# A fused attention and hard-swish kernel on one core: decay terms as columns, scores in halves, and another order of the second batch

## The chip, the core and the metric

The kernel runs on one core of a Trainium2 chip. The metric is the device time of one execution in microseconds (us). Before the change it is 375.04 us, the median of 3 runs (374.90 to 375.15). The profile shown below is of one execution, with a span of 374.1 us. TensorE (PE) multiplies matrices, PEld is its loading of the stationary operand, VectorE is DVE, ScalarE is ACT, GpSimd is POOL, and SP is the engine that issues most transfers.

## The reference, cut to what matters

Eight batches of eight heads each, 576 positions, 64 columns per head. A decay is added to the scores: the cumulative sum of max(s, 0) of the key minus that of the query. Then a causal softmax, and the product with v. The heads of a batch, side by side, are 576 rows of a 4608 x 512 matrix. It goes through two layers, 512 to 2048 and 2048 to 512, with a hard-swish between them.

```python
scores = (1 / np.sqrt(64)) * np.matmul(q, k.transpose(0, 1, 3, 2))
cum = np.cumsum(np.maximum(s, 0.0), axis=-1)
bias = -(cum[:, :, :, None] - cum[:, :, None, :])
scores = np.where(causal, -1e9, scores + np.minimum(bias, 0.0))
attn = softmax(scores)                                # rows sum to 1
x = np.matmul(attn, v).transpose(0, 2, 1, 3).reshape(4608, 512)
h = x @ w_in                                          # 512 x 2048
out = (h * np.clip(h + 3, 0, 6) / 6) @ w_out          # 2048 x 512
```

## The kernel before

Heads are handled in pairs: pair p has the heads 2p and 2p+1, and a batch is four pairs. For each pair q and k are loaded, cast to f16, transposed on TensorE and copied to `qkT`, 64 rows of data and 64 more rows. These extra rows carry the decay in three f16 parts, and rows of a table that keep masked blocks small. In the first pairs the decay rows come from a scan over all 64 heads:

```python
nc.sync.dma_start(out=s_sb, in_=s.rearrange("b h t -> (b h) t"))
nc.vector.tensor_scalar(out=s8, in0=s_sb, scalar1=0.0, scalar2=8.0, op0=ALU.max, op1=ALU.mult)
nc.vector.tensor_tensor_scan(out=c8, data0=s8, data1=s8, initial=0.0, op0=ALU.add, op1=ALU.max)
# ... [cut: c8 split into three f16 parts on DVE]
for hh in range(2):                                   # pair 0: row by row
    nc.sync.dma_start(out=kT[64:65, 0, c0:c1], in_=kaug[hh:hh + 1, 0, :])
    nc.scalar.dma_start(out=qT[67:68, 0, c0:c1], in_=qaug[hh:hh + 1, :])
    # ... [cut: two more parts]
# pairs 1 to 9: the rows go out to a scratch in DRAM and come back by load_aug(p)
```

Pairs 10 to 31 have the decay as columns beside q and k (`xb`, `decay_columns`), and a transpose by DMA. The scores of a head go through four PSUM banks, each with one exp on ACT and one mask on POOL. `attend` multiplies with v, in 15 matmuls of 65 columns. For an odd head it also divides by the row sums.

```python
def scores_bank(hd, bi):                              # four times per head
    S = psum.tile([128, 512], F32, tag="S", bufs=3)
    # ... [cut: one or two matmuls into S]
    nc.scalar.activation(out=P[:, p0:p0 + n], in_=S[:, 0:n], func=AF.Exp, scale=0.125, bias=0.0)
    mask(...)                                         # nc.gpsimd.affine_select on P

def attend(hd):
    # ... [cut: 15 matmuls of Pm with v_h into O]
    if hh == 1:
        nc.vector.reciprocal(out=r, in_=Ov[:, :, :, D:D + 1])
        nc.vector.tensor_tensor(out=xs..., in0=Ov[:, :, :, 0:D], in1=r..., op=ALU.mult)
```

A group of layer 1 (`m1(n, f)`) is four matmuls of 512 columns, a relu on ACT and one operation on DVE. A part of layer 2 (`m2(n, t4, part)`) is four such matmuls, and after the fourth part there is a copy and a store. A block n is 512 rows of the matrix, with 16 groups of layer 1 and 16 parts of layer 2.

```python
run(m1_0[:8])
weave(transposes(4) + pause + pause + block0_tasks(4), m1_0[8:14])
weave(block0_tasks(5), m1_0[14:] + m2_0[:4])
weave(block0_tasks(6) + [(decay_columns, 640), (copy_columns, 0)] + block0_tasks(7), m2_0[4:], 0.85)
weave(att_of[0], m1_tasks(1) + m2_of[1][:8])          # block 1; then one stage for each block
```

The first batch (pairs 0 to 3) runs ahead of `run(m1_0[:8])`. `block0_tasks(p)` is the attention of a pair p of the second batch: its eight score banks, the loads and casts for the pairs after it, both attends, the transposes of the next pair, and the transpose of its own result. `weave` spreads attention tasks between tasks of the layers. The layers' weights are loaded and cast by DMAs that POOL issues: w_in in two halves, within the first batch, and w_out in four pieces.

Of the kernel before, what the change touches and what calls it, by code (L numbers as in the profile page):

```python
# [16 lines left out]
def kernel(  # L17
# [33 lines left out]
    psum = ctx.enter_context(tc.tile_pool(name="psum", bufs=1, space=bass.MemoryType.PSUM))  # L51

    def bank():
        return psum.tile([128, 512], F32, tag="M", bufs=2, name="bank")

    ident_dram = nc.inline_tensor(np.eye(128, dtype=np.float16), name="ident_f16")
# [15 lines left out]
    NA = 8  # L72
    aug_drams = [
        nc.dram_tensor("aug_scratch0", (2, 4, NA * SEQ), F16, kind="Internal").ap(),
        nc.dram_tensor("aug_scratch1", (2, 4, (2 * PTD - NA) * SEQ), F16, kind="Internal").ap(),
    ]
# [3 lines left out]
    nc.scalar.preload_act_table_set("natural_log_exp_and_others")  # L80


    ident = cpool.tile([128, 128], F16, tag="c_id")
# [10 lines left out]
        cpool.tile([128, KC, 1024], F16, tag=f"c_win{h}", name=f"w_in{h}") for h in range(2)  # L94
    ]
    w_out_sb = cpool.tile([128, NF, DM], F16, tag="c_wout")


    amask = work.tile([128, 2, SEQ], F16, tag="amask", bufs=1)
    s_sb = work.tile([NH, SEQ], F32, tag="s0", bufs=1)  # L100
    nc.sync.dma_start(out=s_sb, in_=s.rearrange("b h t -> (b h) t"))
    nc.scalar.dma_start(out=amask[64:128], in_=amask_dram.ap().rearrange("i p t -> p i t"))
    nc.scalar.dma_start(out=ident, in_=ident_dram.ap())

    s8 = work.tile([NH, SEQ], F32, tag="s1", bufs=1)
    nc.vector.tensor_scalar(
        out=s8, in0=s_sb, scalar1=0.0, scalar2=8.0, op0=ALU.max, op1=ALU.mult
    )
    c8 = work.tile([NH, SEQ], F32, tag="s2", bufs=1)
    nc.vector.tensor_tensor_scan(  # L110
        out=c8, data0=s8, data1=s8, initial=0.0, op0=ALU.add, op1=ALU.max
    )

    aug = work.tile([NH, 2, 4, SEQ], F16, tag="s3", bufs=1)
    qaug, kaug = aug[:, 0, 3, :], aug[:, 1]
    nc.gpsimd.memset(warm, 0.0)
    nc.gpsimd.memset(aug[:, 0, 0:3, :], 1.0)
    nc.gpsimd.memset(aug[:, 1, 3, :], 1.0)
# [13 lines left out]
    def mask_rows(sl, copy):  # L132
        for i, dst in enumerate((kT, qT)):
            copy(
                out=dst[64:128, sl, 0:W2].rearrange("p (h t) -> p h t", h=2),
                in_=amask[64:128, i:i + 1, :].to_broadcast([64, 2, SEQ]),
            )


    qk_f = {}  # L140
    qk_h = {}
# [620 lines left out]
```

The softmax here doesn't subtract the row's maximum and nothing guards it: scores larger than these inputs give would overflow.

## Time and profile before

| engine | busy us | share of the span | instructions |
|---|---|---|---|
| PE | 354.2 | 95% | 2805 |
| PEld | 220.5 | 59% | 2805 |
| DVE | 190.4 | 51% | 331 |
| ACT | 209.8 | 56% | 405 |
| POOL | 149.1 | 40% | 378 |

| event | us from the start |
|---|---|
| first scores | 12.84 |
| last attend of the first batch begins | 33.21 |
| first group of layer 1 | 35.30 |
| transposes of pair 4 | 43.13 |
| first group of block 1 | 85.13 |

In the profile's lines a group of instructions is named by engine and line, then output <- inputs and the count. "bank L423" is layer 1, "po" or "bank L450" layer 2, "S L291" scores, "O L340" attend, "pT L247" transposes of q and k, "L378" transposes of the result, "pD L201" those of the decay, and "bank L490" matmuls with zeros that keep TensorE occupied. In the windows each row is a stretch of time, with each engine's busy time in it and, in brackets, the number of instructions; then the clock granted to TensorE, the share of time that the DMA engines were busy, and GB/s. In the waits, three numbers stand for the total in us, the count, and the longest. In the chain of work that ended last, a line is start, us, and what ran. A busy TensorE is not TensorE at its peak, since ends of matmuls are modelled and the matmuls overlap.

### The profile page before, as it was taken

The numbers are of one execution on the slowest core, as the hardware profiler recorded it, in microseconds if no ns is written. First come the engines' busy times: TensorE is split into PE (matmuls) and PEld (weight loads), VectorE is DVE, ScalarE is ACT, GpSimd is POOL, SyncE is SP. The second block draws the span as 40 slices with busy tenths as digits, with TensorE's granted clock in tenths as the row PEclk, the third lists the DMA queues.
The fourth block names the chain that finished last, engine by engine and source line by source line (L and its number), as shares of the span: only waits on it lengthen the run. The fifth ranks groups of instructions, "written<-read, shape, count | busy, mean of one in ns | idle before, by whom it ended". The sixth has DMA issues, their size and how long they took to land.

```text
span 374.1 us, 7656 instructions
## 1 busy us (share of the span) xinstructions
PE 354.2 (95%) x2805; PEld 220.5 (59%) x2805; DVE 190.4 (51%) x331; ACT 209.8 (56%) x405; POOL 149.1 (40%) x378
## 2 busy tenths in 40 slices
PE   6878879999999899999999999999999999999996
PEld 2455556556666566566656665666566655555544
DVE  5765856566642355345534553455345535554431
ACT  4464764336885677467746774677467714553310
POOL 5673344454666344444444444444444300000000
PEclk9999999999999999999999999999999999999999
DMA  9689999938899999899999989899995200011012
GB/s 162 137 155 210 205 218 204 237 108 180 157 190 197 231 172 235 188 232 198 198 208 222 206 177 234 194 196 180 213 194 112 56 31 28 28 39 46 28 58 84
DMA packets 184670, 59.36 MB, mean 159 GB/s; under 512 B 177856, under 2 KB 178336, under 8 KB 184632
## 3 DMA queue, kind: packets, MB, share of 16 engines
q1 hardware_dynamic: 182392, 54.28, 70.2%
q0 software_dynamic: 1680, 4.27, 6.4%
q8 instruction: 22, 0.36, 0.4%
q10 hardware_dynamic: 560, 0.32, 0.3%
q14 instruction: 16, 0.13, 0.1%
HBM read 37.49 MB, written 9.62 MB: 126 GB/s over the span
## 4 chain that ended last, share of the span: by engine, by line
PE 81%; DVE 5%; ACT 4%; DMA 4%; issue 2%; POOL 1%; SPq 1%; ACTq 0%; POOLq 0%
PE bank L423 26%; PE po L450 23%; PE S L291 10%; PE bank L450 7%; PE O L340 6%; PE bankS L423 4%; ACT Pm L299 3%; DMA qkT<-xb 2%; ACT trl L431 1%; DMA qkf<-in_k_dram 1%; DVE gT L432 1%; DVE qkT L262 1%; PE bank L490 1%; PE bankY L423 1%; DMA s_sb<-in_s_dram 1%
## 5 line engine op out<-in xcount | busy, mean ns | idle before, releaser
L299 ACT ACTIVATE Pm<-S 128x384 f16<-128x384 f32 (+2 forms) x256 | 115.5, 508 | 58.4 <-PE S L291 56.6
L432 DVE SCALAR_TENSOR_TENSOR gT<-trl,bank 128x512 f16<-128x512 f32 x123 | 84.5, 687 | 102.2 <-ACT trl L431 101.9
L304 POOL TENSOR_SCALAR_AFFINE_SELECT Pm<-Pm 128x128 f16<-128x128 f16 (+2 forms) x256 | 79.4, 312 | 132.7 <-ACT Pm L299 122.7
L431 ACT ACTIVATE trl<-bank,bias 128x512 f32<-128x512 f32 x123 | 85.2, 692 | 77.3 <-PE bank L423 75.5
L423 PE MATMUL bank<-xT,w_in 128*128 128x512 f16 x492 | 126.4, 382 | 0.7
L450 PE MATMUL po<-w_out_sb,gT 128*128 128x512 f16 x416 | 104.3, 379 | 0.0
L423 PEld LDWEIGHTS <-w_in 128*128 128x128 f16 x576 | 78.5, 146 | 33.3 <-issue 2.4
L450 PEld LDWEIGHTS <-gT 128*128 128x128 f16 x560 | 50.7, 98 | 46.8 <-issue 0.3
L291 PE MATMUL S<-qkT 128*128 128x320 f16 (+4 forms) x448 | 70.2, 261 | 6.8 <-ACT Pm L299 3.4
L291 PEld LDWEIGHTS <-qkT 128*128 128x128 f16 x448 | 41.0, 98 | 36.4 <-issue 3.6
L340 PEld LDWEIGHTS <-Pm 128*128 128x128 f16 x960 | 38.3, 97 | 13.4 <-POOL Pm L304 1.8
L340 PE MATMUL O<-v_h,Pm 128*128 128x65 f16 x960 | 40.8, 193 | 1.5 <-POOL Pm L304 1.3
L450 PE MATMUL bank<-w_out_sb,gT 128*128 128x512 f16 x144 | 35.8, 379 | 0.0
L352 DVE TENSOR_TENSOR xs<-O,r 128x640 f16<-128x640 f32 x32 | 26.4, 824 | 1.1
L459 DVE TENSOR_SCALAR osb<-po 128x512 f32<-128x512 f32 x26 | 17.9, 688 | 15.2 <-PE po L450 14.9
L222 POOL CAST xb<-qkf 128x1152 f16<-128x1152 f32 x22 | 25.3, 1150 | 0.0
L238 POOL CAST v_h<-v_f 128x640 f16<-128x640 f32 x28 | 20.2, 720 | 3.0 <-DMA v_f<-in_v_dram 3.0
L459 DVE TENSOR_SCALAR osb<-bank 128x512 f32<-128x512 f32 x9 | 6.2, 691 | 23.2 <-PE bank L450 23.2
L176 POOL CAST t<-qkf 128x1152 f16<-128x1152 f32 x10 | 11.5, 1154 | 13.7 <-DMA qkf<-in_k_dram 13.7
L423 PE MATMUL bankS<-xT,w_in 128*128 128x512 f16 x64 | 16.4, 379 | 0.0
L431 ACT ACTIVATE trl<-bankS,bias 128x512 f32<-128x512 f32 x16 | 11.0, 688 | 8.0 <-PE bankS L423 8.0
L432 DVE SCALAR_TENSOR_TENSOR gT<-trl,bankS 128x512 f16<-128x512 f32 x16 | 11.0, 688 | 6.8 <-ACT trl L431 6.8
(55 smaller groups left out, 130.8 us busy)
## 6 DMA issues: line engine op xcount, KB each, us to landing
qkf<-in_q_dram SPq DMA_DIRECT2D x32, 288.0 KB, 4.2
qkf<-in_k_dram SPq DMA_DIRECT2D x32, 288.0 KB, 4.3
out_dram<-osb SPq DMA_DIRECT2D x35, 256.0 KB, 2.4
v_f<-in_v_dram SPq DMA_DIRECT2D x64, 128.0 KB, 4.0
w_in<-in_moe_w_in_dram POOLq DMA_DIRECT2D x2, 1024.0 KB, 12.8
w_out_sb<-in_moe_w_out_dram POOLq DMA_DIRECT2D x4, 512.0 KB, 7.3
v_f<-in_v_dram SPq DMA_DIRECT2D x32, 32.0 KB, 2.7
qkT<-xb SPq DMA_TRANSPOSE x22, 4.9
```

What stands on the lines that cost most here:

```text
L222: nc.gpsimd.tensor_copy(out=x.rearrange("p (i t) c -> p t i c", i=2)[:, :, :, 0:D], in_=qk_f.pop(p))
L238: copy(out=v_h[:, sl, :, :, 0:D], in_=v_f[:, sl])
L291: nc.tensor.matmul(out=S[:, c:c + hi - lo], lhsT=kT[:, sl, off + 128 * kt:off + 128 * (kt + 1)], rhs=qT[:, sl, off + lo:off + hi], start=( ...
L299: nc.scalar.activation(out=P[:, p0:p0 + n], in_=S[:, 0:n], func=AF.Exp, scale=0.125, bias=0.0)
L304: nc.gpsimd.affine_select(out=view, in_=view, pattern=pattern, compare_op=ALU.is_ge, fill=0.0, base=0, channel_multiplier=-1,)
L340: nc.tensor.matmul(out=O[:, hh, qt * VW:qt * VW + D + 1], lhsT=P[:, c:c + 128], rhs=v_h[:, sl, hh, kt, 0:D + 1], start=(qt == 0), stop=(qt ...
L352: nc.vector.tensor_tensor(out=xs.rearrange("p t h d -> p h t d"), in0=Ov[:, :, :, 0:D], in1=r.to_broadcast([128, 2, 5, D]), op=ALU.mult,)
L423: nc.tensor.matmul(out=ph, lhsT=w_in_t[f // 8][:, kc, f % 8, :], rhs=xT[:, kc, n * 512:(n + 1) * 512], start=(kc == 0), stop=(kc == KC - 1),)
L431: nc.scalar.activation(out=trl, in_=ph, func=AF.Relu, bias=bias3[:, 0:1], scale=1.0)
L432: nc.vector.scalar_tensor_tensor(out=gT[n][:, f, :], in0=trl, scalar=6.0, in1=ph, op0=ALU.min, op1=ALU.mult)
L450: nc.tensor.matmul(out=po, lhsT=gT[n][:, f, t4 * 128:(t4 + 1) * 128], rhs=w_out_sb[:, f, :], start=(f == 0), stop=(f == NF - 1),)
L459: nc.vector.tensor_scalar_mul(out=osb, in0=po, scalar1=1.0 / 6.0)
```

## The change

The aim is to start the first batch sooner, to take masks and small transfers out of it, and to have layers 1 and 2 of block 0 in another place. The parts:

- **Decay of the first batch as columns.** Only s of batch 0 is loaded at first, as 72 rows of 64. One short scan and four small matmuls with 0/1 tables give the cumulative sums, already transposed. They are written as columns beside q and k in a tile `x0`, and come out of the transposes as rows 64 to 67. The scan over all heads comes later, on POOL and DVE, for pairs 4 to 9 and the columns of the later pairs.
- **Scores in halves.** A head of the first batch has two halves of 896 and 704 columns, each over two PSUM banks with one exp. The causal mask is one more matmul for each diagonal block, of the identity with a triangle of -65504.
- **Weights in quarters.** w_in comes as four DMAs of 512 columns, and all eight weight DMAs are issued while head 5 is worked on. The columns of one stationary operand of w_in are now 4 elements apart, not 8.
- **Second batch beside layer 2.** All of layer 1 and the first half of layer 2 of block 0 run ahead of the second batch, without attention beside them. The second batch has the other 8 parts of layer 2.
- **PSUM by hand.** One tile of eight banks, with rings of bank numbers, in place of tagged tiles. Layer 1 of block 0 has a ring of six.

```diff
+    XW = 68
+    x0 = gT2[:, 1]...                       # [cut] pair, tile, q or k, 68 columns
+    def first_columns():
+        nc.vector.tensor_scalar(out=s_first, in0=s_first, ...)
+        nc.vector.tensor_tensor_scan(out=scan, data0=s_first, data1=s_first, ...)
+        # [cut] four matmuls with `sums` into cT
+        nc.vector.tensor_copy(out=hi, in_=c3)
+        nc.vector.tensor_tensor(out=r3, in0=c3, in1=hi, op=ALU.subtract)
+        # [cut] mid, lo and the negative of hi in the same way
+    def scores_half(hd, half):
+        # [cut] three matmuls of k and q, two or three of ident and tri
+        nc.scalar.activation(
+            out=Pm[:, hd % NS, p0:p0 + n], in_=S[:, 0:n], func=AF.Exp, scale=0.125, bias=0.0
+        )
-    w_in_t = [w.rearrange("p k (m f) -> p k f m", f=8) for w in w_in_sb]
+    w_in_t = [w.rearrange("p k (m f) -> p k f m", f=4) for w in w_in_sb]
-        copy = nc.vector.tensor_copy if p < 4 else nc.gpsimd.tensor_copy
-        copy(out=v_h[:, sl, :, :, 0:D], in_=v_f[:, sl])
+        nc.gpsimd.tensor_copy(out=v_h[:, sl, :, :, 0:D], in_=v_f[:, sl])
+    keep_warm(6)
+    first_columns()
+    mask_rows(0, 1, A.copy)
+    mask_rows(0, 0, G.tensor_copy)
+    # [cut] casts and turns of pair 0 in two pieces, on A, G and V
+    for hd in range(2 * FIRST):
+        scores_half(hd, 0)
+        # [cut] turn_first of q or k of the next pair, cast of the pair after it, loads
+        scores_half(hd, 1)
+        if hd > 0:
+            attend(hd - 1)
+        if odd and p > 0:
+            x_transpose(p - 1)
+        if hd == 5:
+            for c in range(4):
+                load_w_in(c)
+            for c in range(4):
+                load_w_out(c)
+    rows = decay_rows()
+    rows[0]()                                # POOL: memsets, product
+    attend(2 * FIRST - 1)
+    opened = [bank("A") for _ in range(4)]
+    # [cut] groups 0 to 3 of layer 1: kc 0 to 2 around x_transpose(3), then kc 3 and m1_act
+    rows[1]()                                # DVE: scan over all heads
+    rows[2]()                                # POOL: three f16 parts
+    store_aug(nc.sync)
+    for sl in (1, 2, 0):
+        for i in range(2):
+            mask_rows(sl, i, G.tensor_copy)
+    for p in range(FIRST, FIRST + 3):
+        load_pair(p)
-    run(m1_0[:8])
-    weave(transposes(4) + pause + pause + block0_tasks(4), m1_0[8:14])
-    weave(block0_tasks(5), m1_0[14:] + m2_0[:4])
+    run(m1_0[4:])
+    run(m2_0[:8])
+    cast_qk(FIRST)
+    cast_v(FIRST)
+    weave(transposes(4) + block0_tasks(4), m2_0[8:10])
+    weave(block0_tasks(5), m2_0[10:13])
     weave(
         block0_tasks(6) + [(decay_columns, 640), (copy_columns, 0)] + block0_tasks(7),
-        m2_0[4:],
+        m2_0[13:],
         0.85,
     )
```

## The prediction

> **What bounds the kernel now.** I read the windows first, cut at the borders of the stages, because the 95% of TensorE over the span hides where its idle time lies.
>
> ```profile
> core 0: us, PE busy (x) PEld busy (x) DVE busy (x) ACT busy (x) POOL busy (x), PEclk, DMA share, GB/s
> 0.00:12.80 12.80, 8.81 (x38) 3.72 (x39) 8.46 (x14) 4.17 (x4) 6.82 (x14) 1.00 0.78 133
> 12.80:35.30 22.50, 17.43 (x234) 12.37 (x233) 14.34 (x30) 13.32 (x32) 13.86 (x36) 1.00 0.92 181
> 35.30:43.10 7.80, 7.80 (x39) 5.08 (x37) 5.28 (x8) 5.44 (x8) 1.23 (x2) 1.00 0.93 188
> 43.10:85.10 42.00, 36.88 (x364) 23.38 (x364) 26.39 (x62) 19.08 (x41) 20.86 (x46) 1.00 0.94 197
> 85.10:122.40 37.30, 36.66 (x340) 24.43 (x339) 18.90 (x32) 27.15 (x57) 22.21 (x58) 1.00 0.96 175
> ...
> 160.10:197.90 37.80, 37.66 (x311) 23.84 (x310) 17.77 (x29) 24.49 (x48) 18.35 (x49) 1.00 1.12 212
> ```
>
> From 85.1 us on TensorE is full (37.66 of 37.80 us), and the change leaves that code alone but for the weights' layout. So the question is only when block 1 of layer 1 starts. Before that there are 12.8 us without scores, 22.5 us of the first batch, and 42 us of the second batch woven with layers 1 and 2 of block 0, where 5.1 us are idle. The waits of TensorE up to 36 us, and the longest early pieces of the chain, come second:
>
> ```profile
> PE pTm L247 <- POOL t L176: 2.7, 2, 1.7
> PE S L291 <- ACT Pm L299: 1.4, 6, 0.3
> ```
>
> ```profile
> 17.01 1.16 POOL t L176
> 18.27 5.15 DMA qkf<-in_k_dram
> 23.54 1.15 POOL t L176
> 32.51 0.86 PE bank L490 x4
> 35.47 1.79 PE bank L423 x8
> ```
>
> The first batch is held by GpSimd's cast of a pair, and that by a q/k load (5.15 us of the chain), while each head has four exps and four masks in sequence. Third, the timeline of TensorE from the attends of pair 6 to block 1, because it shows what a pair costs when little is woven in:
>
> ```profile
> 69.12 0.83 PE L340 MATMUL O<-v_h,Pm 128*128 128x65 f16 x15
> 69.80 1.02 PE L450 MATMUL bank<-w_out_sb,gT 128*128 128x512 f16 x4
> 70.66 0.67 PE L247 MATMUL pT<-ident,t 128*128 128x128 f16 x9
> 71.16 0.44 PE L378 MATMUL pT<-ident,xs 128*128 128x128 f16 x5
> 71.44 1.03 PE L450 MATMUL po<-w_out_sb,gT 128*128 128x512 f16 x4
> 72.63 0.65 PE L201 MATMUL pD<-ident,aug 64*128 64x64 f16 x10 [0.16 <-DVE qkT L262]
> 73.51 1.14 PE L201 MATMUL pD<-ident,aug 64*128 64x64 f16 x20 [0.23 <-DVE qkT L262]
> 74.58 1.04 PE L450 MATMUL po<-w_out_sb,gT 128*128 128x512 f16 x4
> 75.49 0.33 PE L291 MATMUL S<-qkT 128*128 128x256 f16 x2
> ...
> 85.13 1.03 PE L423 MATMUL bank<-xT,w_in 128*128 128x512 f16 x4
> ```
>
> [...] the 384-wide exp takes 494 ns, the 512-wide 598 ns, and four in a row (1600 columns) end 1.69 us after the first begins. [...] a group of four stands in the chain with 0.86 us. [...] Here 98 ns hold for gT, qkT and Pm, but 146 ns for w_in, whose columns lie 8 elements apart[...]. [...]
>
> **The change, part by part.**
>
> Start. The decay terms of pair 0 no longer go through row DMAs (the eight small ones are issued at 6.7 to 10.6 us) but come from one scan and four small matmuls into columns of x0. Only 18 KB of s are loaded for it, so I put those columns at about 5.6 us. The mask load is now third on its queue: I put it at 5.3 us (it ended the wait of ACT's mask copy at 4.66). Then on ACT a mask copy (1.15), a cast of about 0.45, five transposes and a copy of about 0.5 us on VectorE; ACT's k copy is about 0.7 us, later by a little. First scores at 8.4 instead of 12.84 us.
>
> First batch. Per head two exps of 896 and 704 columns[...]. The 1.5 us of masks on GpSimd go. TensorE gains two or three small matmuls per half for masks: scores take 0.48 + 0.43 us plus some gaps, about 1.0; attend 0.47 (15 in the chain); nine transposes for q or k 0.5; x_transpose 0.28. That is 2.0 us for an even head, 2.3 for an odd one, with turns; 1.5 and 1.7 in the last pair, whose successor is turned later. The sum without waits is some 16 us. The loads decide the middle: 4 pairs of 885 KB plus about 0.4 MB at the 205 GB/s that busy stretches show land pair 2's q and k at 13.5 us, pair 3's at 17.8, the last v at about 21. With a 1.15 us cast pair 3 is turned at 19; three and a half heads follow, so 26. GpSimd issues eight weight DMAs from about 20 (0.55 to 0.77 us each, 5 us) before it casts the v of pair 3, done at 25.7, when attend of head 6 wants it: up to 0.8 us. So layer 1 starts at 27 instead of 35.3, and the bubble after the last attend (1.17 us on xs) is filled by the four opened sums. Gain here: 8.3 us.
>
> Layer 1 of block 0 with half of layer 2, alone: 24 groups of 0.864 us, 20.7, so 48. Weights: the two halves landed 10.6 and 15.0 us after issue; a quarter at a time at that pace comes every 3 to 4 us from 23.5, and w_out is in by about 45. Both ACT and VectorE need 0.69 us per group, under 0.864, and six banks give slack for the scan (1.35) inserted on VectorE. GpSimd meanwhile: aug memsets and product 2.8, wait for the scan until about 35[...], six mask copies of 1.15 = 7, then casts 1.15 + 0.72: 48.4. This only just meets TensorE at 48.
>
> Second batch. It now has 8 groups of layer 2 beside it (6.9 us) instead of 23 (19.9). A pair has attention of about 3.7 us on TensorE, but its own chain is longer: first score to last attend 5.2 us (64.79 to 69.96, with one group inside), then reciprocal, xs and the first two copies of q and k on VectorE, 2.6 us (70.00 to 72.6), and the next scores. That is 7.8 us a pair where the woven groups fall into holes. Now it takes 9.7. Pair 4 also pays transposes and copies at its head, 2.4 us, so scores at 50.4. Pairs 5 and 6 begin at 58.3 and 66.7 (one group lies on the path in each). The decay columns lengthen pair 6 to pair 7: 5.5 us lie between 69.96 and 75.49, so pair 7 begins at 77.3. It needs 5.0 to its last attend, then a group, transposes and x_transpose, 2.0. Block 1 begins at 84.3 instead of 85.1. Idle TensorE in this stage: 36.3 us less 6.9, four times 3.7 and 1.5 of decay transposes, so 13 us, against 5.1 in the old stage.
>
> Sum. Of 8.3 us gained, some 7.5 are given back, because 15 groups have been moved out of the holes of the second batch. The weights' columns lie 4 elements apart instead of 8. Where a layer-1 group follows scores or attends it takes 0.90 us in the chain instead of 0.86; about half of the woven groups do. If the load gets shorter, up to 0.04 x some 70 = 2.8 us come over the rest of the kernel; I take half, 1.4, plus the 0.8: 2.2 to 3. Predicted: 372.0 us.
>
> **The rivals.** First: the early start survives. If woven groups, shorter waits of the pairs, or an x_transpose off the path hold the second batch to 31 us, block 1 starts at 79 to 80 and the time is near 368; a stride-free weight load takes it to 366.5. For it speaks that the S banks and ACT have no relu beside them now; against it that pair 6 of before already ran with few groups and still needed 5.2 + 2.6 us. Second: GpSimd becomes the bound. It carries casts of v that VectorE did, row operations, six mask copies and eight DMA issues; the 1.58 us of one VectorE subtraction that took 0.75 alone shows that they can disturb each other. If its chain ends at 52 instead of 48.4, all that follows moves: 375 to 376. Third: the transfers. DMA stands at 0.92 to 0.94 busy up to 85 us, so nothing done earlier helps if bytes arrive no sooner. But pairs 4 to 6 are asked for at about 40 us with the queue free, and pair 7 some 15 us later. Weights late by 5 us would give 377.
>
> **Range and chances.** The start of layer 1 I trust to 1.5 us, the second batch to 3, the weight load to 1.4; together about 3.6, leaning to the fast side. Range 366.5 to 377.5. Faster by over 2% means under 367.5, which needs nearly the whole early gain: 0.15. Slower by over 2% means over 382.5, two of the rivals against me: 0.05. Within: 0.80.
>
> **What the profile will show.** Right: first scores at 8 to 9 us, no affine select in the first batch, layer 1 from 26 to 28 us, then 20 us of full TensorE, then about 36 us at some 65% busy, block 1 at 83 to 86, and stages of 37.7 us or a little less after it, with weight loads of w_in under 146 ns. Wrong: block 1 near 80, TensorE waiting for the weights' DMA or for a GpSimd cast near 48, or waits in the later stages.

## The result, and the profile after

The changed kernel takes 376.79 us (median of 4 runs, 376.26 to 377.87) against 375.0 for the kernel before (4 runs, 374.9 to 375.15): ratio 1.0047, 95% interval 1.0029 to 1.0064. It is slower by half a per cent, where 0.8% faster had been predicted.

In what follows "block 1" as a moment is the start of the first group of layer 1 of block 1, and so on for the other blocks. A "hole" is a stretch in which TensorE waits for the chain of one pair, and in which a woven group can run. In the new kernel's lines L488 is layer 1, L527 layer 2, L330 scores of the second batch and later, L396 scores of the first batch, L418 attend, L286 transposes of q and k, L456 those of the result, L247 those of the decay, L567 zero matmuls. First the windows of the changed kernel, cut at its own borders (first scores, layer 1, block 1, block 2, block 3), columns as before:

```profile
core 0: us, PE busy (x) PEld busy (x) DVE busy (x) ACT busy (x) POOL busy (x), PEclk, DMA share, GB/s
0.00:10.22 10.22, 6.50 (x28) 2.76 (x28) 4.71 (x13) 3.58 (x4) 4.75 (x15) 1.00 0.93 183
10.22:28.75 18.53, 18.00 (x286) 15.10 (x287) 10.08 (x18) 12.96 (x16) 14.73 (x19) 1.00 1.00 188
28.75:84.68 55.93, 48.37 (x409) 28.11 (x406) 31.59 (x69) 23.77 (x48) 32.23 (x55) 0.97 0.89 186
84.68:123.29 38.61, 35.25 (x323) 21.50 (x321) 20.61 (x37) 26.98 (x56) 21.54 (x58) 1.00 0.83 164
123.29:160.88 37.59, 37.42 (x316) 21.91 (x312) 17.76 (x29) 24.48 (x48) 18.50 (x49) 1.00 1.17 217
```

The first batch starts 2.6 us sooner and TensorE is full in it (18.00 of 18.53 us): layer 1 starts 6.5 us sooner. From there to block 1 it takes 55.93 us instead of 49.83, with 7.6 us of idle TensorE instead of 5.1. The next row has 3.4 us of idle TensorE (35.25 of 38.61 us busy), in a stage that the prediction took to be full. The timeline of TensorE in the changed kernel shows where:

```profile
30.37 12.68 PE L488 MATMUL PS<-xT,w_in 128*128 128x512 f16 x58
43.68 7.93 PE L527 MATMUL PS<-w_out_sb,gT 128*128 128x512 f16 x36 [0.63 <-DVE gT L499]
51.45 0.67 PE L286 MATMUL PS<-idtri,t 128*128 128x128 f16 x9
52.98 0.56 PE L330 MATMUL PS<-qkT 128*128 128x256 f16 x4 [0.86 <-DVE qkT L301]
...
77.59 0.33 PE L330 MATMUL PS<-qkT 128*128 128x256 f16 x2 [0.76 <-DVE dec L262]
78.40 0.59 PE L330 MATMUL PS<-qkT 128*128 128x192 f16 x2 [0.48 <-DVE dec L260]
...
84.68 0.81 PE L488 MATMUL PS<-xT,w_in 128*128 128x512 f16 x3
87.24 0.38 PE L488 MATMUL PS<-xT,w_in 128*128 128x512 f16 x1 [1.75 <-DVE xT L464]
```

Four things stand in it. Layer 1 and half of layer 2 run without attention beside them from 28.75 to 51.45, with one gap between the layers. The two scores of 192 columns, 0.38 us elsewhere (at 90.66), take 0.59 at 78.40, where the granted clock is one half (0.50 in the windows, from 78.3 to 81.7). Block 1 begins at 84.68, but its fourth matmul comes at 87.24: it reads the transposed result of pair 7, whose copy stands on VectorE behind the four copies of pair 8. So block 1 really begins some 1.75 us later than its first line says. The borders of the traces, in us, beside those of two kernels from the experiments below:

| kernel | layer 1 | block 1 | block 2 | block 3 | span |
|---|---|---|---|---|---|
| before | 35.30 | 85.13 | 121.00 | 159.96 | 374.1 |
| after | 28.75 | 84.68 | 123.29 | 160.88 | 374.3 |
| e16_win | 30.27 | 84.44 | 121.28 | 158.87 | 372.0 |
| e18_ahead | 29.20 | 81.56 | 120.07 | 157.66 | 370.8 |

From block 3 on nothing differs but the weights' layout. (Before it, each kernel has waits of its own: before stands for 1.03 us at 125.3 for a transfer of `xb`, so block 3 is the border to compare.) The changed kernel is 0.92 us behind there and regains 0.75 by the end. (The profiled execution of before is a long one: a median of 375.0 less the 1.7 us that time and span differ by is 373.3.)

### The profile page after: what moved, and what is told of

Read it like the earlier page. It is cut to its first block, busy times and chain, and to the rows that moved or that the text cites. A ratio compares the mean times of both kernels' runs of the same rounds, so it can differ in the third digit from the quotient of the medians.

```text
span 374.3 us, 7691 instructions
## 1 busy us (share of the span) xinstructions
PE 355.0 (95%) x2852; PEld 206.8 (55%) x2852; DVE 184.0 (49%) x322; ACT 207.8 (56%) x389; POOL 158.3 (42%) x368
## 4 chain that ended last, share of the span: by engine, by line
PE 83%; ACT 5%; DVE 5%; issue 3%; DMA 2%; POOL 1%; POOLq 0%; ACTq 0%; DVEq 0%
PE PS L527 31%; PE PS L488 30%; PE PS L330 9%; PE PS L418 6%; ACT Pm L338 3%; DVE qkT L301 2%; PE PS L396 2%; DMA qkf<-in_q_dram 2%; ACT trl L498 2%; PE PS L732 2%; DVE gT L499 1%; PE PS L456 1%; PE PS L547 1%; POOL Pm L343 1%; PE PS L286 1%
## 5 line engine op out<-in xcount | busy, mean ns | idle before, releaser
L499 DVE SCALAR_TENSOR_TENSOR gT<-trl,PS 128x512 f16<-128x512 f32 x144 | 97.8, 685 | 105.7 <-ACT trl L498 105.6
L488 PE MATMUL PS<-xT,w_in 128*128 128x512 f16 x576 | 143.0, 379 | 2.6 <-DVE xT L464 1.7
L498 ACT ACTIVATE trl<-PS,bias 128x512 f32<-128x512 f32 x144 | 98.4, 691 | 81.7 <-PE PS L488 79.0
L527 PE MATMUL PS<-w_out_sb,gT 128*128 128x512 f16 x560 | 138.2, 379 | 0.6 <-DVE gT L499 0.6
L338 ACT ACTIVATE Pm<-PS 128x384 f16<-128x384 f32 x224 | 102.1, 507 | 57.0 <-PE PS L330 55.4
L343 POOL TENSOR_SCALAR_AFFINE_SELECT Pm<-Pm 128x256 f16<-128x256 f16 x224 | 68.8, 307 | 126.2 <-ACT Pm L338 117.5
L488 PEld LDWEIGHTS <-w_in 128*128 128x128 f16 x576 | 61.5, 114 | 46.3 <-issue 2.4
L527 PEld LDWEIGHTS <-gT 128*128 128x128 f16 x560 | 51.0, 98 | 49.3 <-issue 0.9
L330 PE MATMUL PS<-qkT 128*128 128x256 f16 x392 | 63.4, 265 | 5.2 <-DVE qkT L301 2.9
L330 PEld LDWEIGHTS <-qkT 128*128 128x128 f16 x392 | 36.9, 99 | 39.0 <-issue 9.3
L418 PEld LDWEIGHTS <-Pm 128*128 128x128 f16 x960 | 38.4, 98 | 13.6 <-POOL Pm L343 2.8
L536 DVE TENSOR_SCALAR osb<-PS 128x512 f32<-128x512 f32 x35 | 24.1, 688 | 43.3 <-PE PS L527 43.0
L418 PE MATMUL PS<-v_h,Pm 128*128 128x65 f16 x960 | 41.3, 193 | 2.2 <-POOL Pm L343 1.9
L430 DVE TENSOR_TENSOR xs<-PS,r 128x640 f16<-128x640 f32 x32 | 26.4, 824 | 1.1
L396 PE MATMUL PS<-qkT 128*128 128x64 f16 (+4 forms) x48 | 9.6, 292 | 1.0 <-ACT qkT L738 0.8
## 6 DMA issues: line engine op xcount, KB each, us to landing
w_out_sb<-in_moe_w_out_dram POOLq DMA_DIRECT2D x4, 512.0 KB, 16.5
```

The costliest lines, as they stand in the source:

```text
L330: nc.tensor.matmul(out=S[:, c:c + hi - lo], lhsT=kT[:, sl, off + 128 * kt:off + 128 * (kt + 1)], rhs=qT[:, sl, off + lo:off + hi], start=( ...
L343: nc.gpsimd.affine_select(out=view, in_=view, pattern=pattern, compare_op=ALU.is_ge, fill=0.0, base=0, channel_multiplier=-1,)
L418: nc.tensor.matmul(out=O[:, hh, qt * VW:qt * VW + D + 1], lhsT=P[:, c:c + 128], rhs=v_h[:, sl, hh, kt, 0:D + 1], start=(qt == 0), stop=(qt ...
L430: nc.vector.tensor_tensor(out=xs.rearrange("p t h d -> p h t d"), in0=Ov[:, :, :, 0:D], in1=r.to_broadcast([128, 2, 5, D]), op=ALU.mult,)
L488: nc.tensor.matmul(out=ph, lhsT=w_in_t[f // 4][:, kc, f % 4, :], rhs=xT[:, kc, n * 512:(n + 1) * 512], start=(kc == 0), stop=(kc == KC - 1),)
L498: nc.scalar.activation(out=trl, in_=ph, func=AF.Relu, bias=bias3[:, 0:1], scale=1.0)
```

## The experiments

Ratios are against the kernel before, run beside it on the same chip. The medians of the kernel before lie between 374.9 and 376.7 us from one experiment to another, and single runs spread over several us, so small effects are read from the borders in the traces. The trace of e10_half is of an execution that took 382.26 us, the longest of 14, so its borders are not compared.

**The start: is it TensorE's slow pace?** e1_warm doubles the zero matmuls that keep TensorE occupied.

```diff
-    keep_warm(6)
+    keep_warm(12)
-    keep_warm(4)
+    keep_warm(8)
```

> The changed kernel with 12 and 8 matmuls on zeros at the start instead of 6 and 4. Theory A (TensorE ran its first work at half clock: its 512-wide matmuls are 0.43 us apart up to 13.6 us and 0.22 after it): the first scores begin near 9.5 instead of 10.2 us, the 17 transposes after them take about 1.0 instead of 1.8 us, layer 1 begins 1.5 to 2.2 us sooner, at about 27, and the time falls to 374.6 to 375.3. Rival (the start waits for q, casts and loads whatever the clock is): layer 1 begins within 0.4 us of 28.9 and the time stays at 376.4 to 377.

Measured: ratio 1.008 [1.0051, 1.0109], first scores at 10.80, layer 1 at 29.06. The timeline of e1_warm:

```profile
6.63 0.45 PE L709 MATMUL PS<-sums,scan 72*64 72x36 f32 x4
...
9.22 0.75 PE L732 MATMUL PS<-idtri,gT 128*68 128x128 f16 x10
10.80 0.39 PE L396 MATMUL PS<-qkT 128*128 128x512 f16 x1 [0.83 <-ACT qkT L738]
```

The ten transposes take 0.75 us instead of 1.28. (In after a zero matmul of 512 columns takes 634 ns, one of layer 1 379; from the first scores at 10.22 to the next matmul it is 0.40 us, from those at 13.63 it is 0.22. The windows give a granted clock of 1.00 for this stretch too, so a half clock at the start is read from these times alone.) But all of them now stand behind zeros: the matmuls of the decay columns at 6.63 instead of 4.47, the transposes at 9.22 instead of 8.11. A pace that is bought in this way does not bring layer 1 forward; with it, layer 1 comes 18.26 us after the first scores instead of 18.53.

**The border between the layers.** The first part of layer 2 took a bank that a group of layer 1 still held (1.45 us between the last layer-1 and the first layer-2 matmul). e2_ring turns the ring of banks so that it is free.

```diff
-    "A": (3, 4, 5, 0, 1, 2)
+    "A": (5, 3, 4, 0, 1, 2)
```

> The changed kernel with the ring of layer 1 of block 0 turned by one place, so that the first sum of layer 2 gets a bank whose group was finished three groups earlier. Theory B (the 1.45 us between the last matmul of layer 1 at 42.2 us and the first of layer 2 at 43.68 is the wait for a PSUM bank that the last but one group holds): TensorE goes on without a gap, pair 4's transposes come 1.2 to 1.4 us sooner, unless GpSimd's cast (ends at 50.2 us) holds them, and the time falls by 1.0 to 1.4 us to about 375.5. Rival (layer 2 waits for the last gT itself): no change of the gap, 376.4 to 377.

Measured: ratio 1.0003 [0.9977, 1.0029]. Layer 2 follows without a gap at 43.20, and the transposes of pair 4 come 21.9 us after layer 1's start (50.97 less 29.05) instead of 22.7. It gives back 0.8 us.

**The copy ahead of block 1.** e3_xt puts the transposes of pair 7's result ahead of those of pair 8.

```diff
-            + transposes(p + 1)
-            + [(lambda: x_transpose(p), 640)]
+            + ([(lambda: x_transpose(p), 640)] + transposes(p + 1) if p == 7
+               else transposes(p + 1) + [(lambda: x_transpose(p), 640)])
```

> The changed kernel with the transposed result of pair 7 ahead of the transposes of pair 8. Theory C (the first group of block 1 stands 1.75 us because its last input is copied by VectorE behind four copies for pair 8): that wait goes, block 1 runs 1.0 to 1.8 us sooner, time 375.0 to 375.8. Rival (pair 8's scores then wait for the copies that have moved back, so nothing is gained): 376.3 to 377.

Measured: ratio 1.0035 [1.0008, 1.0063]. The wait of 1.75 is gone and the stage from block 1 to block 2 takes 37.10 instead of 38.61, but block 1 itself starts 0.5 later after layer 1 (56.4 against 55.9), since it now waits on the result itself. Net 1.0 in the trace; too little to show in the times.

**The weights' layout alone.** e4_quarters is the kernel before with w_in in four tiles, so that a matmul's columns lie 4 elements apart instead of 8.

> The kernel before with w_in in quarters, columns of a stationary operand 4 elements apart, and nothing else of the change. Theory D (the weight loads of w_in, 146 ns before and 114 ns after, are exposed where a group follows scores or attends): 1.0 to 2.0 us faster than before, 373.0 to 374.0, with stages of about 37.5 instead of 37.75 us. Rival (the loads lie under matmuls anyway, and what the changed kernel has gained behind block 1 has another source): 374.8 to 375.2.

Measured: ratio 0.9986 [0.9962, 1.0009]; stages of 37.59 instead of 37.75, span 373.31 instead of 374.10. The group of weight loads in before, then in e4_quarters (busy, then ns of one, then idle time):

```profile
L423 PEld LDWEIGHTS <-w_in 128*128 128x128 f16 x576 | 78.5, 146 | 33.3 <-issue 2.4
```

```profile
L420 PEld LDWEIGHTS <-w_in 128*128 128x128 f16 x576 | 61.3, 114 | 45.9 <-issue 2.9
```

The loads are busy for 17.2 us less in all, and the span is 0.8 shorter: nearly all of it lay beside matmuls. The interval of the ratio includes 1; what speaks for the 0.8 is that each stage is shorter by the same 0.16.

**The half clock.** e6_fill puts zero matmuls where TensorE is thin: seven and seven at the start, four after the decay columns, two and two about an attend of pair 6. e8_after is the changed kernel once more, beside it.

> The changed kernel with matmuls on zeros where TensorE idles: 7 and 7 instead of 6 and 4 at the start, and two each around the second attend of pair 6 and four after the decay transposes. Theory F (the halved clock costs time: it was granted at half up to 13.4 us and from 78.3 to 81.7): the clock is full from about 8 us on with no half stretch before the end, the transposes of pair 1 take about half as long, pair 7 from first score to last attend takes 4.7 instead of 5.45 us, and block 1 starts 1 to 2 us sooner. Rival (those stretches wait for loads, casts, exps and copies, and the clock does not matter there): block 1 starts within 0.5 us of 84.7 counted from the same start of layer 1, or later by what the zeros add.

> The changed kernel once more, unchanged, beside the three others and the kernel before: 0.3 to 0.7% above the kernel before, layer 1 from 28.8, block 1 from 84.7 us. It shows how far its stage borders and clock repeat.

Measured: e6_fill 1.0051 [1.0007, 1.0096], e8_after 1.006 [1.0019, 1.01]. In the traced run of e6_fill the granted clock from layer 1 to block 1 is 0.97, as in after, and block 1 comes 57.1 us after layer 1 instead of 56.0. Four other runs of e6_fill show a full clock (1.00) and took 376.13 to 377.16 us, where five runs of e8_after at 0.995 took 376.24 to 379.32, four of them 376.43 or less. So a full clock with zeros shows no gain; what the half clock costs by itself is not shown. The repeated kernel has a granted clock of 0.995 over its traced run, as after has. It also has a wait that the first trace of the same kernel lacks, near the end of block 1:

```profile
120.76 0.56 PE L330 MATMUL PS<-qkT 128*128 128x256 f16 x4 [1.48 <-DMA qkT<-xb]
```

It is for the transposed columns of a later pair, and the stage from block 1 to block 2 is 40.25 us long, against 38.61. The traces of e1_warm (1.6 us) and e18_ahead (1.5 us) have such a wait too.

**The order of the layers alone.** e7_order is the kernel before with the change's order: all of layer 1, eight parts of layer 2, then the second batch with the other eight. First batch and rows stay as they were; the four loads of the weights of layer 2 are asked for ahead of the casts of pair 4.

```diff
-    run(m1_0[:8])
-    weave(transposes(4) + pause + pause + block0_tasks(4), m1_0[8:14])
-    weave(block0_tasks(5), m1_0[14:] + m2_0[:4])
+    run(m1_0)
+    run(m2_0[:8])
+    weave(transposes(4) + block0_tasks(4), m2_0[8:10])
+    weave(block0_tasks(5), m2_0[10:13])
     # [cut] the last weave takes m2_0[13:] instead of m2_0[4:]; order of the w_out loads
```

> The kernel before with one part of the change alone: all of layer 1 and half of layer 2 of block 0 run ahead of the second batch, 8 parts are woven in. (The four weight DMAs of w_out are issued ahead of pair 4's casts, so that they are in time.) Theory E: block 1 starts 5.5 to 7 us later than in the kernel before, at 90.5 to 92 us, and the time is 5.5 to 7 us above that of the kernel before in the same job. Rival (the order of the layers costs little, the second batch gets shorter by what is taken out of it): block 1 within 2 us of 85.1.

Measured: 384.91 us, ratio 1.0254 [1.0182, 1.0326], from two runs (386.72, which is the traced one, and 383.10); block 1 at 95.15 instead of 85.13, with stretches in which four matmuls of 512 columns take 1.90 us (at 64.88) instead of 1.03. Its window from layer 1 to block 1, and its first group of block 1:

```profile
35.52:95.15 59.63, 52.08 (x399) 31.34 (x400) 30.04 (x65) 24.75 (x48) 19.70 (x43) 0.89 0.79 165
97.57 0.38 PE L423 MATMUL bank<-xT,w_in 128*128 128x512 f16 x1 [1.60 <-DVE xT L386]
```

In this trace the order costs 9.8 us (59.63 against 49.83), more than the 5.5 to 7 expected; half clock (0.89 granted over the stretch) is a part of it that I hadn't reckoned with, and the other run was 3.6 us shorter. So this part of the reasoning holds in kind: taking the groups out of the holes eats the early start. And the kernel before, with this order alone, also stands for 1.60 us in its first group of block 1: the wait needs the order and no other part of the change.

**GpSimd's chain.** The change copies the masks into rows 64 to 127 of the q and k slots a second time, 6.60 us on GpSimd. Rows 68 to 127 still hold them from the first batch, and rows 64 to 67 are loaded over. e11_nomask leaves those six copies out.

> After with the six repeated mask copies left out (6.60 us on GpSimd between the decay rows and the casts of pair 4), nothing else. If GpSimd's chain sets the start of the second batch (my second rival, and its casts at 49.1 and 50.2 came just ahead of the transposes at 51.4): pair 4 starts up to 1.5 us earlier and block 1 at 83 to 84, time down by 1 to 1.5. If TensorE's order sets it (layer 1 and half of layer 2 back to back): transposes of pair 4 again at 51 to 52, block 1 at 84.5 to 86, time within 0.4 us of after.

Measured: ratio 1.0059 [1.0032, 1.0086]. Transposes of pair 4 at 52.35, layer 1 at 29.64: 22.7 us between them, as in after. The cast of pair 4 then waits for its loads instead (to 48.68). The second rival, GpSimd as the bound of the changed kernel, is out.

**The groups woven back, first attempts.** If leaving the holes empty costs the gain, filling them should return it. e5_weave works the rows out during the first batch, asks for pairs 4 to 6 right away, and weaves all 16 parts of layer 2 into the second batch. e9_woven asks only for pair 4 ahead of the rows, leaves the repeated masks out, and weaves in 7 groups of layer 1 as well. e10_half has the same feed with layer 1 ahead. All three carry e2's ring and e3's order. The cut of e9_woven:

```diff
-    run(m1_0[4:])
-    run(m2_0[:8])
-    weave(transposes(4) + block0_tasks(4), m2_0[8:10])
-    weave(block0_tasks(5), m2_0[10:13])
+    run(m1_0[4:9])
+    run(transposes(4))
+    weave(block0_tasks(4), m1_0[9:14])
+    weave(block0_tasks(5), m1_0[14:] + m2_0[:4])
```

> The changed kernel with all 16 parts of layer 2 woven into the second batch instead of 8. For that the decay rows of pairs 4 to 9 are made earlier (memsets after head 2, product and scan on VectorE at head 5, the rest on GpSimd during layer 1), pairs 4 to 6 are loaded earlier, pair 4 is cast and transposed within layer 1; the ring of e2_ring and the order of e3_xt are in it too. Theory E (the early start is given back because groups that lay in the holes of the second batch now run alone): the holes take eight more parts, 6.9 us of work; the second batch begins near 43 instead of 51.5 us and block 1 near 79.5 to 80.5 instead of 84.7 (with its first wait, 86.4), and the time is 370 to 372. Rival (the second batch is as long as its own work and waits, or loads and weights between 20 and 50 us bound it): block 1 not before 83, time 374 to 377.

> After with the ring of banks (5, 3, 4, 0, 1, 2), the transposed output of pair 7 ahead of the transposes of pair 8, and: the rows of the decay for the second batch worked out during the first batch; pair 4 of q, k, v loaded ahead of the weights of layer 2 having landed, the rows stored and loaded back ahead of pairs 5 and 6; the six repeated mask copies (6.60 us on GpSimd; rows 68 to 127 of the slots still hold the masks of the first batch) left out; only 9 groups of layer 1 ahead of the second batch, and the other 7 groups with all 16 parts of layer 2 (23 groups of 0.86 us) woven into its four pairs instead of 8. Theory (the gain was given back because 16 groups stand ahead of the second batch instead of in its holes): TensorE's own work from the start of layer 1 to block 1 is 24 groups, 20.7 us, and the second batch's own, 33.4 minus 8 groups and its waits, some 17 to 18; with a tenth of waits block 1 starts 43 to 50 us after layer 1 does, at 74 to 80 instead of 84.7 (86.4 with its wait), no half-clock stretch, and the time is 369 to 371.5. Rival (it was feeding, not order: the weights, 4.2 MB in SBUF, keep the DMA engines full to 45, and pairs 5 and 6 or the weights of layer 2 arrive too late): TensorE waits for qkT, casts or w_out between 40 and 60, block 1 no earlier than 84, 375 or more.

> The same feed as the woven kernel (rows early, pair 4 early, no repeated masks, ring, order at pair 8), but all 16 groups of layer 1 ahead of the scores of pair 4 and only the 16 parts of layer 2 in the second batch: a middle dose between 8 groups (after) and 23. Theory: the eight parts of layer 2 that now lie ahead of the second batch (6.9 us) go into its holes (TensorE idle there for some 10 us); scores of pair 4 at 44 to 45, block 1 at 79 to 82, 370.5 to 373; it stands between after and the woven kernel. Rival (feed): as late as after, 84 to 87, or later than the woven one by nothing.

Measured: e5_weave 1.0314 [1.028, 1.0347], e9_woven 1.0032 [1.0007, 1.0057], e10_half 1.0026 [0.9995, 1.0057]; block 1 at 97.34 in e5_weave and 87.01 in e9_woven. The rival's reading, late transfers, came true, and not only for pairs 5 and 6: it is the rows of pair 4 that come late. The timeline of TensorE in e9_woven:

```profile
39.28 1.02 PE L488 MATMUL PS<-xT,w_in 128*128 128x512 f16 x4 [0.22 <-DVE gT L499]
46.59 2.07 PE L330 MATMUL PS<-qkT 128*128 128x256 f16 x9 [6.29 <-DMA qkT<-aug_scratch]
```

and its DMA issues on SyncE:

```profile
33.85 0.34 SPq L572 DMA_DIRECT2D aug_scratch<-aug  x1
41.73 0.27 SPq L215 DMA_DIRECT2D qkT<-aug_scratch  x1
```

The rows of the decay, 108 KB, go to DRAM at 33.85 and are there only at 41.6; their way back, 18 KB, takes to 46.6. The DMA engines are busy throughout (a share of 1.13, 1.06 and 0.94 in the three windows of 5 us from 35 to 50), with the weights of layer 2 among others: asked for at 23.4 to 25, a median of 20.7 us to landing, and read by nobody before 59.85. TensorE stands for 6.3 us and then runs at half clock to 49.5 (granted 0.77 from 40 to 45, 0.55 from 45 to 50). In e5_weave pair 5 and 6 stood in the same queue ahead of the rows too, and the wait was 11.9.

**The weights of layer 2 later.** e12_late is e9_woven with these four loads moved behind the casts of pairs 4 and 5, and a few groups moved one stage back.

```diff
-            for c in range(4):
-                load_w_out(c)
...
     cast_v(FIRST)
+    load_w_out(0)
+    load_w_out(1)
...
+            if p == 4:
+                load_w_out(2)
+                load_w_out(3)
```

> The woven kernel with the four loads of the weights of layer 2 issued later: two after the casts of pair 4 (some 36 instead of 23 to 25), two after those of pair 5; 4 more of layer 1 in pair 4, 3 and 2 parts of layer 2 in pair 5, the other 14 parts in pairs 6 and 7. In the woven kernel the store of the rows took from 33.85 to 41.6 and their way back to 46.6, among 2.1 MB of weights of layer 2 that no one read before 59.8, and TensorE stood 6.3 us. Theory (what keeps the second batch out of the first 16 us after layer 1's start is the early load of these weights; the layers were put ahead of it to fill that time, and this gives the early start back): the rows are back at 38 to 39, scores of pair 4 at 38.5 to 40, no wait over 1.5 us, block 1 at 76 to 81, stages 37.6, time 368.5 to 371.5, under both kernels. Rival (the DMA engines as a whole, or the engines beside TensorE, bound this stage): the wait moves to pair 5 or 6 or to the weights of layer 2 (TensorE waits 3 us or more for casts or w_out between 45 and 65), block 1 at 83 to 87, time 373.5 or more.

Measured: 375.63 us, ratio 0.9983 [0.9947, 1.0018]. Scores of pair 4 come at 40.90 without a wait for rows, as expected; block 1 at 85.77, as the rival said. The wait has moved to pair 5, whose loads are issued at 38.3, behind the store. TensorE and the windows of e12_late:

```profile
49.42 0.68 PE L286 MATMUL PS<-idtri,t 128*128 128x128 f16 x9 [3.09 <-POOL t L222]
```

```profile
35.00:40.00 5.00, 4.79 (x30) 2.58 (x27) 4.90 (x9) 4.05 (x7) 1.86 (x3) 1.00 0.38 84
45.00:50.00 5.00, 1.78 (x28) 1.32 (x27) 2.17 (x5) 1.11 (x3) 2.32 (x5) 1.00 1.03 228
```

The DMA engines had been 0.38 busy just before, with SyncE's queue held up by the rows.

**Pairs 4 to 6 in order, the rows through GpSimd's queue.** e13_pair5 and e14_win were the first form; in them the loads of pair 6 overwrote pair 3's v ahead of its cast, so that pair 3 used the v of pair 6 and TensorE waited 20.2 us for it. They say nothing of the question. e15_pair5 and e16_win have those loads behind that cast; e16_win also asks for half of w_in 1.3 us earlier. In all four the 16 parts of layer 2 lie in pairs 6 and 7.

```diff
+            for i in range(2):
+                load_qk(FIRST + i, nc.sync)
+                load_v(FIRST + i, nc.sync)
+    load_qk(FIRST + 2, nc.sync)
+    load_v(FIRST + 2, nc.sync)
     rows[2]()
-    store_aug(nc.sync)
-    load_aug(FIRST, nc.sync)
-    load_pair(FIRST + 1)
-    load_pair(FIRST + 2)
+    store_aug(nc.gpsimd)
     cast_qk(FIRST)
     cast_v(FIRST)
+    for i in range(3):
+        load_aug(FIRST + i, nc.gpsimd)
```

> The woven kernel with late weights, and pairs 4, 5 and 6 of q, k, v asked for one after the other ahead of the store of the rows (which, with its way back, goes through GpSimd's queue); the 16 parts of layer 2 all in pairs 6 and 7. In the run before this one the rows were in time (scores of pair 4 at 40.9) but the loads of pair 5 stood behind their store in the queue: asked for at 38.3, landed at 48.2, while the DMA engines were busy 0.38 of the time from 35 to 40, and TensorE idled 3.9 us from 46.3 to 49.4 and then ran 3.4 us at half clock. Theory (the order in which transfers are asked for gives back the early start; with them in order the groups lie in holes): no wait over 1.5 us between 40 and 85, no half clock, block 1 at 79 to 82.5, 369 to 372. Rival (the DMA engines as a whole bound the stage to block 1): the wait moves to w_out or pair 6 (3 us or more), block 1 at 84 to 87, 374 or more.

> The same with half of the weights of layer 1 asked for 1.3 us earlier, ahead of the cast of v of pair 2, in the gap of the DMA engines from 15 to 20 us. If the DMA engines bound the stage to block 1, everything after comes 1 to 1.3 us earlier: block 1 at 78 to 81.5, time 1 us under the run beside it. If TensorE's order and the chain of each pair bound it: no change within 0.5 us.

> The run e13_pair5 with its slip mended: there the loads of pair 6 stood ahead of the cast of v of pair 3, whose buffer they share, so that pair 3 took the v of pair 6 and waited 20 us for it. Here they follow that cast; nothing else is changed. Theory (the order in which transfers are asked for gives the early start back): rows in time, pair 5 landed by 46, no wait over 1.5 us between 40 and 85, no half clock, block 1 at 79 to 82.5, 369 to 372. Rival (the DMA engines as a whole, or the pair's own chain, bound the stage to block 1): the wait moves on, block 1 at 84 to 87, 374 or more.

> The same with half of the weights of layer 1 asked for 1.3 us earlier (e14_win mended). If the DMA engines bound the stage: 1 to 1.3 us earlier everywhere after; if not, within 0.5 us of the run beside it.

Measured: e13_pair5 1.0439 [1.0388, 1.049] and e14_win 1.0408 [1.0361, 1.0455], as told; e15_pair5 375.68 us, 0.9995 [0.9967, 1.0023], block 1 at 84.96; e16_win 374.4, 0.9963 [0.9943, 0.9984], block 1 at 84.44, block 3 2.0 us ahead of after. From layer 1's start to block 1 both take 54.2 us: the earlier request moves layer 1 by 0.5 and no more. The wait for pair 5 is gone, but block 1 is not at the 79 to 82.5 that was expected. What is left is a wait of 2.04 us for the rows at 42.3 in e16_win and half clock from 42.8 to 46.2 (granted 0.78 from 40 to 45, 0.88 from 45 to 50).

**Without the wait.** e17_rows moves one row operation to ScalarE and puts one more group of layer 1 ahead of pair 4; e18_ahead puts 12 groups ahead. The cut of e18_ahead, against e16_win:

```diff
+            nc.scalar.mul(out=qaug, in_=c8, mul=-1.0)
-            g.tensor_scalar_mul(out=qaug, in0=c8, scalar1=-1.0)
...
-    run(m1_0[4:9])
-    weave(block0_tasks(4), m1_0[9:13])
-    weave(block0_tasks(5), m1_0[13:])
+    run(m1_0[4:12])
+    weave(block0_tasks(4), m1_0[12:14])
+    weave(block0_tasks(5), m1_0[14:])
```

> The kernel e16_win with the wait for the rows taken away: one of the five row operations (the negated one, 1.66 us) moved from GpSimd to ScalarE, and one more group of layer 1 ahead of the transposes of pair 4. There TensorE waited 2.04 us for the rows at 40.3 to 42.3 and ran at half clock from 42.8 to 46.2. Theory (late rows are what is left of the loss, and the half clock follows from the wait): scores of pair 4 at 40.5 to 41.5, no half-clock stretch, block 1 at 81 to 83, 371 to 373 and 0.5 to 0.9 per cent under the kernel before. Rival (the pair's own chain fills up whatever is gained): block 1 again at 84 to 85, 374 to 375.

> The same with 12 groups of layer 1 ahead of pair 4 instead of 10, so that fewer lie in pairs 4 and 5: scores of pair 4 at 42.3 to 43, certainly without a wait. If groups in holes are what pays: block 1 some 1 to 1.7 later than in the run beside it. If only the wait and the half clock counted: the same within 0.5.

Measured: e17_rows 374.32 us, 0.9948 [0.9923, 0.9973], block 1 at 83.14, still with 2.42 us for the rows; e18_ahead 371.81, 0.9893 [0.9866, 0.992], without that wait, block 1 at 81.56. The scores of pair 4 in e18_ahead, and its windows, layer 1 to scores of pair 4, then pairs 4, 5, 6 with the decay columns, and 7:

```profile
40.91 1.03 PE L488 MATMUL PS<-xT,w_in 128*128 128x512 f16 x4
42.46 0.56 PE L330 MATMUL PS<-qkT 128*128 128x256 f16 x4 [0.52 <-DVE qkT L301]
```

```profile
28.75:42.30 13.55, 12.84 (x84) 6.95 (x81) 10.36 (x18) 8.24 (x14) 7.54 (x11) 1.00 1.12 216
42.30:50.30 8.00, 5.92 (x67) 3.87 (x67) 4.45 (x10) 4.33 (x10) 5.25 (x12) 1.00 1.15 230
50.30:58.50 8.20, 6.14 (x67) 3.92 (x66) 4.40 (x10) 4.54 (x10) 4.21 (x10) 1.00 1.04 214
58.50:70.00 11.50, 11.09 (x117) 6.75 (x116) 6.62 (x21) 3.60 (x8) 4.22 (x10) 1.00 0.85 199
70.00:81.55 11.55, 10.53 (x92) 5.93 (x90) 6.54 (x19) 3.70 (x8) 5.46 (x11) 1.00 0.49 123
```

All 16 parts of layer 2 lie in pairs 6 and 7, where TensorE is now nearly full; pairs 4 and 5, with two groups each, stay thin (5.92 of 8.00 us). The granted clock is 1.000 over this run. This version is 1.1% faster than the kernel before (its median is of 6 runs). If groups in holes had been what pays, it should have reached block 1 some 1 to 1.7 us later than e17_rows; it came 1.6 earlier. The scores of pair 4 come only 0.4 us later than in e17_rows (42.46 against 42.03), as the two groups fill the time in which it waited, and from there to block 1 it takes 39.1 us instead of 41.1. Taking two groups of 0.86 us out of pairs 4 and 5 shortened these by 2.0 us, so there the two had not lain in holes.

The lead is not kept in the traces. Block 3 comes at 157.60 in e17_rows and at 157.66 in e18_ahead, which stands for 1.50 us within block 1:

```profile
114.48 0.56 PE L330 MATMUL PS<-qkT 128*128 128x256 f16 x4 [1.50 <-DMA qkT<-xb]
```

So both spans are alike (370.7 and 370.8 us). The timed runs of e17_rows lie higher, at granted clocks between 0.98 and 1.00, those of e18_ahead between 0.991 and 1.00; whether the wait brings a half clock in some runs, no run isolates.

## Why the prediction was wrong

**What bounds the kernel.** "The change leaves that code alone", and so "the question is only when block 1 of layer 1 starts": this step failed. Block 1's first matmul came at 84.68, against 84.3 predicted, and still the kernel lost. The border does not say that the stage behind it runs full: block 1's fourth matmul waited 1.75 us for a copy that the new order put behind four others, so the 0.8 us of gain in my sum (0.45 measured) became a loss of 0.92 at block 3. I read the old stage's fullness (36.66 of 37.30) as a property of its code, where it was one of what came just before. e7_order shows that the order alone brings the wait (1.60 us in the old code), and e3_xt shows it to be removable and worth 1.0 net.

**Start.** 8.4 was predicted for the first scores, 10.22 came. The larger mis-sized term is the load of the masks: I put it at 5.3 us, but ScalarE stood for it until 6.43.

```profile
6.43 1.15 ACT L175 COPY qkT<-amask 64x1152 f16<-64x1152 f16 x1 [1.70 <-DMA amask<-amask]
7.60 0.46 ACT L726 CAST gT<-qkf 128x320 f16<-128x320 f32 x1
```

That is 1.1 of the 1.8 us, since the cast and the transposes follow this copy. Nearly all the rest lies between the cast and the scores: 2.2 us (8.06 to 10.22) where I had 1.5, with 10 transposes at 1.28 us and a wait of 0.83 for ScalarE's copy. I reckoned with the pace of the later transposes. But e1_warm, with these at 0.75, shows that more zeros ahead of them don't mend it.

**First batch.** Right in its mechanism: no affine select in it, TensorE full (18.00 of 18.53 us), and the two exps of a head at 0.92 and 0.76 us on ScalarE, less than the 2.3 us a head took. It took 18.5 us where I had 18.6, so layer 1 came at 28.75 instead of 27 by the late start alone. The gain was 6.5 us, not 8.3.

**Layer 1 and half of layer 2 alone.** 21 us were predicted (27 to 48), 22.7 came; e2_ring shows 0.8 of the difference to be one bank in a ring of six.

**Second batch.** Predicted 33.9 us from the scores of pair 4 to block 1, measured 31.7. Pairs 4 to 7 were put at 7.9, 8.4, 10.6 and 7.0 us and took 6.9, 7.6, 10.1 and 7.1 (their scores begin at 52.98, 59.90, 67.51 and 77.59): the chain of a pair was shorter than I had it. The scores came 2.6 us late (52.98 against 50.4), the pairs ran 2.2 us short, and the border came out nearly right by luck. I had also put 13 us of idle TensorE and some 65% busy here:

```profile
51.45:84.68 33.23, 26.30 (x300) 17.16 (x299) 17.57 (x48) 13.75 (x32) 17.13 (x41) 0.95 0.78 174
```

It was 6.9 us idle and 79% busy, a part of it at half clock from 78.3 to 81.7, which I hadn't foreseen. "Given back, because 15 groups have been moved out of the holes" is right in kind: e7_order shows a loss of 9.8 us for the order alone in its trace, half clock included, and its other run was 3.6 us shorter.

**Weights.** The term of 1.4 us for the shorter loads measured 0.8 in e4_quarters, and 0.75 from block 3 on in the changed kernel.

**Sum.** A gain of 2.2 to 3 was predicted. My terms, 0.8 and 1.4, add up to 2.2; the 372.0 took the upper end, for which the sum has no term. In the traced runs the gain became a loss of 0.92 up to block 3 and 0.75 regained behind it. Between the medians 1.8 us are lost: the trace of before is 0.8 above its median, that of the changed kernel is the shortest of four runs, and other runs can have the wait for `xb` that e8_after shows.

**Rivals.** The first (the early start survives) did not happen here, but I had taken the holes to be its only condition. e9_woven shows that weaving back alone brings no gain over the kernel before, since the rows then wait among the weights. With transfers asked for in the order of use, and after several steps more, e18_ahead reaches block 1 at 81.56 and is 4.1 us faster than the kernel before (371.81 against 375.87), of which some 0.8 is the layout. It has 12 groups of layer 1 ahead of pair 4, where the changed kernel has all of layer 1 and half of layer 2. The second (GpSimd) is out for the changed kernel by e11_nomask; its five row operations, for whose time on GpSimd before gave no figure, took 5.53 us in after. The third I had dismissed, as pairs 4 to 6 were asked for "with the queue free"; that was true only because of the order I blamed. The weights of layer 2, asked for at 23 us, take a median of 16.5 us to land in after, the DMA engines are full to about 42 (a share of 1.16 from 23 to 41, 0.22 from 42 to 43), and the change fills that time with layer 1 and half of layer 2.

What stays open: what brings the half clock on; whether another number of groups ahead would do better than 12; why the wait for `xb` comes in some runs and not in others; and what the later transfers would bring with the changed kernel's own order of the layers, which was not run.

## What to carry to other kernels

When a stage is moved forward, move its transfers by order of use, not all of them forward: in e9_woven loads whose data was first read some 35 us after their issue were under way while the next stage stood 6.29 us for a transfer of 18 KB. Before blaming an order of work, ask what its inputs wait for in the order you would prefer; here weaving alone brought no gain, and the gain came with both changed; the transfers alone were not tried. And a predicted border is not yet a predicted time: look at what the first instructions behind it read.

## What the runs showed of the hardware that was not expected

The half clock came without long idle times. In after it was granted from 78.3 to 81.7, and no wait of TensorE from 51 us to there exceeded 0.9 us; in e16_win it stood from 42.8 to 46.2, right behind a wait of 2.04 us. Yet e17_rows had a wait of 2.42 us and, in its profiled run, a granted clock of 1.00. Thin work went before it in after (TensorE busy 7.64 of 10.80 us, 67.5 to 78.3), but e18_ahead was nearly as thin (5.92 of 8.00, 42.3 to 50.3) at 1.00. What decides on it, these runs don't show.

A small DMA among large ones was slow on its way: the store of 108 KB took 7.8 us with the weights of both layers asked for (4.2 MB in SBUF, e9_woven) and 4.1 with those of layer 1 alone (e12_late).

The time of a weight load of 128 x 128 f16 grew with the distance of its columns: 98 ns side by side (gT in before), 114 at 4 elements (w_in in e4_quarters and after), 146 at 8 (w_in in before).
